# GpSimd issues the output stores of batches 1 to 7; the planner's SyncE lengths and its two strings are new

## The chip, the core and the metric

One core of one Trainium2 chip runs the whole program. The metric is device microseconds from start to end of one execution; smaller is better. The core has TensorE (matmul, "PE"), VectorE ("DVE"), ScalarE ("ACT"), GpSimd ("POOL") and SyncE ("SP"). SyncE, ScalarE and GpSimd issue the transfers, and sixteen DMA engines carry them. In the profile's rows, q1 is the ring of SyncE's transfers and q0 that of GpSimd's.

## The reference

Two layers follow each other on 8 batches of 3136 rows: a gated attention with squared ReLU in place of softmax, and a Hyena layer with an FFT convolution along the sequence.

```python
scores = (1.0 / S) * np.matmul(z, z.transpose(0, 2, 1))   # z: 8 x 3136 x 64
attn = np.maximum(scores, 0.0) ** 2
x = u * np.matmul(attn, v)                                # u, v: 8 x 3136 x 256
proj = x @ w_proj                                         # 256 -> 768
x1, x2, x3 = proj[..., :D], proj[..., D:2 * D], proj[..., 2 * D:]
x2_conv = np.fft.irfft(np.fft.rfft(x2, n=S, axis=1) * H, n=S, axis=1)
out = (x1 * x2_conv * x3) @ w_out                         # float32, 8 x 3136 x 256
```

H is the transform of `filter_fft`. S is 3136 = 64 x 49 and D is 256.

## The kernel before

All matmuls are in bfloat16 with float32 sums. The sequence is cut into seven chunks (`CHUNKS`: five of 512 rows, one of 256, one of 320), with rows laid out in the order that factors the Fourier transform into two small matrix products (64 x 49).

**Attention.** For each batch and chunk, TensorE makes scores between the chunk's rows and 128-row tiles of all rows (two tiles at a time, into a pair of PSUM banks; four such pairs exist). ScalarE or VectorE takes the ReLU into R_t (lines 1919 and 1921) and the square into A_t (1928 and 1930). TensorE weighs v with A_t and sums over the tiles. Since the scores are symmetric, a block made for one chunk is also needed, transposed, by a later one: `mirror` has SyncE transpose A_t into M_t, M2e_t or M2o_t by DMA (line 1848). At a chunk's end VectorE multiplies the sum with the transposed u (uT_t) into xT_t (line 1975).

**Loads.** GpSimd loads u, v and z and casts them to bfloat16 on the way (lines 621 to 656, into un_t, v_t, zn_t). It is paced: ahead of each load it copies one element of a finished tile (`tick`, lines 636 and 639), so that it waits until that tile is done. SyncE then transposes un_t into uT_t (line 1565) and the doubled z into zT_t (line 1620).

**Hyena.** From xT_t TensorE makes the three projections. The product of the first and third is the gate (gate_t, line 1256). The second goes through the first Fourier factor (`dft1`) and SyncE writes it to a DRAM scratch (`spec`, lines 1028 and 1031). When a batch's seven chunks are there, SyncE reads them back turned (spec_in_t, line 1062, three transfers per load), TensorE does the second factor, VectorE multiplies with H (xh, lines 1357 to 1362), TensorE transforms back (gs_t), and SyncE writes the result to the scratch (line 1406, three transfers each). `add_end` then handles one chunk at a time: SyncE loads conv_in_t (line 1091), TensorE finishes the inverse transform, VectorE applies the gate (yT_t, line 1462), TensorE multiplies with w_out, ScalarE or VectorE copies the float32 result into ost_t (lines 582 and 586), and a store goes to `out_dram` (line 1511). ost_t has two tiles. A store is two transfers, one for each half of the partitions.

**Order.** The program is one long straight list. While it is built, a planner (`Plan`) runs a clock: each piece of work is a `Task` with the engine, a planned length, what it depends on and which buffers it takes. A task with `moves` is a transfer: it lands later by its share of the DMA work, of which the planner keeps two heaps, SyncE's and GpSimd's; `late` is added to the landing. For SyncE, GpSimd, ScalarE and VectorE the planner picks the task that can start first on its clock (then the lower `prio`, then the older), and that fixes each engine's order of issue. For TensorE the order is written out in the string `ORDER`: one letter per piece (S scores, w and v the two halves of a weighing, A projections and first factor, Q spectrum, B the end of a batch, Z work kept for the last batch). The string `ENGINES` says for each piece that ScalarE (a) or VectorE (d) could do, which of them does it. All engines run in order, and each waits on semaphores for what it needs.

So the Hyena part of one batch is laid into the attention of the next. The stores of batches 0 to 5 are SyncE's; those of batch 6 are GpSimd's, four of them and three more inside the last batch; the last batch (7) divides its stores over GpSimd, SyncE and ScalarE. (The code counts batches from 0; batches 1 to 7 of the title are its 0 to 6.)

Of the kernel before, what the change touches and what calls it, by code (L numbers as in the profile page):

```python
# [27 lines left out]
LATE_U, LATE_ZT = 0.5, 2.0  # L28
# [28 lines left out]
    "vwSSwQwQAvAvSAvvwSAvwvSvwwwSvvQwwwSvSQvwAvQAvASvAQwwvSwvQwASAwvSwSwSvwASvSAwvAwSAvSwwwAvvASAvvAvvSSw"
    "wwSAvSAwvvSvASwAwwSBSBvwvSAvASwBvSBvAwAwABvBAwSvSwvAwAvSAvwSwwABSBwSvvAwAASAvwBvSBwAwABSwBvSvvSvvSwB"
    "ABvAwwSvwSwSAvBwABvvvSSwAwASvBvwBSwwAvSASwvwvBSBvwvASwAwwASAvQwvSQwvvSvQwwSQvwQvwQvSAvBABwAwBSAvBvvw"
    "SvSwwAASAwAvSvQwSwQwvSQvvvQwBwBwASvASwvwvSwwSvQvvwwvQSwwBvwSvBSvAvASAwASwvSSvvwQwQAvAwwvSASvSAwAQAwS"  # L60
    "wwQwSvASAvvwSwvvvSSvwvwvvwSAwSwASvwSvvAwBASBvwSwvSSwBvABvABvBwBwSBvSwvSAvwAwwSAvSAwvAwSAvBvBSvwSvAAA"
    "wABSwBwBAwwwBAAvAAvASvSvvvBABwASwwSwASAAvvSAvwvSBvSwwSwBSwSvwvSvSAvAvBQBwAvQwAvwQvwSvSQwAwwQAvvSvwQQ"
    "wwSvwAQvSAwvSwSvBwvSBvwvSAwAvvQSwBwBwQwBQvBQvvSvQwSSvwASwAvSvAwwAAwwvAvSvwwAvvwSvSAwSvwSwvBSwBAvSwAS"
    "vQSvwvvASwASwwwSQvvAwSSAwvSvwASvvSwwQwAvASAvwvvSvwwSAwASvvvwSSAvwAwAwSBABvvBwBSBwvSAvBAvSwAwASvvSBwS"
    "BvwwBwABvASvvSAwAwSSwBwBAvAASwAwBvBAAAvABSwvBSvwSvvSSvwBvBwwAwAvSSwwvvwAAAwSAvwSAvASSvwwvwSSQvvBwBQv"
    "vBSvBwwSvwAwAvwSSvAwAQvQvwSvQAwBABQwwvSvSQwBvwBAQAvSvvAQAwwAwQAvwSSvSwwvSSwAvvvSwQAvQwvSwQwwBSvQBvvS"
    "wvwwAvSvvwSvwwSAvQvwQvwSSvwSvAwSASvwAwSSAwwAwSASwvwvSSwvAwAvSAvASwwAvAvSvvSvwwvSwSvAvvAwBSBwvBwSBBBv"
    "wSvSAvAwwSSvvwSwSBvBwAvASvwwwSwBvBSAvAvvwwSwAAAAAvASwvSASwvBABSvvwSAvASwwwSwvwvvwSvSwvSSAwABvwvSwBSv"
    "wwSwSvwSBvBBvvBSvwvwASvAvwSwSAwASvAvAvSwASAwAvAQwvQwBvSwBQAwAwSvQAvwAwwQvvQvwSvQwABwBAQvwSvSQvvSwwQw"
    "BvSBvQvvSwSwwwvSvvvwwSAvSvAwwwSQvSvvSAwAvwSAvASASAQwSwwwQvSwQvASwASwvvwSwAvASvvwQSwwvAvAvSvvwSwwSABw"  # L70
    "BAvSvvSABABAwAwSSvvSvwASwASvwBSwBvwAwSAvSvAvAvSwBvwSBwAwAwAwSBABvvSAwAvSAwABSBwBvSvwBSvvvwSAvAAwABvB"
    "vwSwwSvSBwBvBvSwBvAwSAAvwSAwvSwBAwAwBAvASvvSwSAvASvAvAQwwSwQvwAQAvSwwwvSvASvwBASBvvwBQBvSwwQAwSAvSQv"
    "vvQwwSwSQwwwBvBQAvvASQvwSwwQvvwSQvvQwvSBwvSBvAvAAwAvwSSvwwwASAvvSwwwSQAwAvSQvvvSSvAwAwwSSwwwSASvAwSv"
    "wSvvQwSvvwASvwvAAwSvvAvvwSwwSAwSAvvBwSBBwBSvAwAvSSvwSwABvSABvwSBwSvBvwvSSBvBAvAwwwSABwABvvSvSBvBSwwA"
    "AAASvAwASAvAwSAwAwBSvBBvBwSvwSvwwSwSvvSvwvASwAwSwwBSvSBwwQQvSvvwQSvAvwQAvBvQBvwwvQAwAwwQwQSvwvSSvvvB"
    "BvBBvwSwASwwSAvSvwSvvSwvvAwASwSvwvBSvwwBQwQAvSAwvQwSvwQQvwSvwAQvSAvwvwBvSvwBwwASAwvvSSwvAQvwAvSwQvvS"
    "wwwSSvAwASvwwZvSZAwAvSvvwwwZwwZvvvvvvZZABABZZAABBBBZZZZBZBZBZZZZBQQQQBQQQBQQQQQZZQQZQZQZZZZZBZBZZZBZ"
    "BBZBBZBZBBBBBZBBBBBZZZZBBBBBBBBBBBBBB"
# [3 lines left out]
    "aadddddddaaddaaaaaaddaaaddaadaadaadadadadaaaadadaddadddaaaadaadaaddaadaadaaddaddaaaaaaaaadadaddaddad"  # L82
    "aaaadadaaadaddadadaaaadddaaadaaaaddaddaaaaddaaadadddaaaaaaadadaaaaaadddaaadadaaaaaaaaadaaaaaddaadadd"
    "aaddaadadaaaadadadaddaaadaaadaaddaddadadaaddadadaadaaaddaadaaaadaddaaaaaddddadaaadaaaaaddaadaaaaaada"
    "addadaadaddaaadadaaaadaaaadaadaaaaddddaadadaaaaaaadaaaaddaaadaaadddaadaadaaadadadaaadddaaadaaaadddad"
    "adaaaaadddadadadaaaadaaaadddaaaaaaddaadaddaadaaadaaaaaadadaaddaaaaaadaaadaaadaadaaaaaaaadaaddaaaaaaa"
    "aaaaaaaadddadadadaaadadaadaaaaaadaaaaaaaaaaaaadddaaddaaaadadaddadaaaaadddaaaadddaaaddaaaddaaaaaaaaaa"
    "dadaaaadaddaaadaadddaaaaadaaadaddadadaaaaaaadadaadaaaaadaaadadadaaadaadaadddaddaadaaddaadadaddadadaa"
    "adadaaaaadaaaaaddadadaddaadaaaadaadaaadaaadadadaaadadaaaaadddaadaaaadaaaaaaddadddaaaadaadaaaddaaaaad"
    "aaaaaadaaaaaaaaaadaddadaddaaaadaaaaadaadadddaaaddaaddaaaaddadaadaaddaaaadaaaaddaaaadaaaaaadadaddaada"  # L90
    "aaaaaddadaadadadadaaaaddaaadadaaddadadaaaadadaaddadadaaaaaaaddadadaaaddaaddaaaaaadaaaadaaaaaaadadaad"
    "adaaaaadadadaddadadaaaddaaadaaaaadaaaaaaaaaaadaaaaaaaaadaaaadddaaddadaadaadaaaadadaddddadaaaaadaddda"
    "adaaaadddaaddaaaaaaaaaaddaaaddaadaadaaadaadaadaaaadadaadaddaaaadaddadaaaaadaaadadaaaaadaddadaaaadaaa"
    "addddaddadaaaadaadaadaaaadaaadaaaadaddadaaddaaadddaaaaaaaaddaadadadadddadaaaaaaaadaaadadadaaaaddaada"
    "dddaaadaaadaaaadaaaaaddaadaddaaaddaaadaadaadaddaaaaaadddaaadaadaadddaaddaaaadadaaddaaaaaaadaaaaaaaaa"
    "aaaaaaaadaaaaaaaaaaadadaad"
# [3 lines left out]
ISSUED = "issued"  # L100
# [286 lines left out]
def kernel(  # L387
# [188 lines left out]
    def on(engine, emit, cost, deps=(), takes=(), **kw):  # L576
        return job(None, lambda e: emit(), {engine: cost}, deps, takes, **kw)
# [420 lines left out]
    def dft1(kind, get, t0, nt, dst, deps, free=None, late=0.0, split=False):  # L998
# [40 lines left out]
        c = on("SP", put, 0.5 * (1 + (nt == 3)), [b_], moves=0.254 * nt, late=late)  # L1039
# [5 lines left out]
    def in_order(task):  # L1045
        loads.append(task)
        return task
# [8 lines left out]
    def load_spec(src, j0, nj, deps, late=0.4, home=l_p):  # L1056
        box = {}

        def go():
            box["t"] = home.tile([P, 8, D], BF16)  # L1060
            for rows, part in by_row(src, box["t"], 2 * j0, 2 * nj):
                nc.sync.dma_start(out=part, in_=rows)
# [21 lines left out]
    def load_c(src, c, deps, home):  # L1084
# [8 lines left out]
        if home is c_p:  # L1093
            return in_order(on("SP", go, 0.55, [*deps, *((d, ISSUED) for d in loads[-1:])], [home.slots], moves=0.254 * nt, late=LATE_C)), box
# [224 lines left out]
    def add_spectrum(b, puts, early=0):  # L1319
# [10 lines left out]
        for g in range(NJ // 2):  # L1330
# [41 lines left out]
            def inv(g=g, xb=xb, z_=z_, a0=a0, gh=gh, mine=mine, per=per):  # L1372
# [41 lines left out]
                else:  # L1414
                    p_ = on("SP", put, 1.5, gx["es"], moves=0.389 * per, late=LATE_D2)
# [10 lines left out]
    def add_end(b, lasts, gtasks, cs, kind="FB", src=c_p, dsts=(o_p,), late=0, behind=(), then=(), split=False, mids=(y_p,)):  # L1426
        for at, c in enumerate(cs):
# [92 lines left out]
            elif b == B - 2:  # L1520
# [40 lines left out]
    def load_uT(b, c, deps):  # L1561
# [9 lines left out]
        if not isinstance(made[0], Task):  # L1571
            t = after(on("SP", go, 1.3, deps, [uT_p.slots], moves=0.2 * u_tiles(c), late=LATE_U), made[1])
# [497 lines left out]
```

## Time and profile before

| | |
|---|---|
| three runs | 950.38, 957.36 and 955.5 us; median 955.5 |
| profiled execution | span 944.1 us from the first to the last instruction; its own time with what lies around the span is not listed |
| granted TensorE clock | 0.997 of full speed |
| HBM | read 90.26 MB, written 53.05 MB |
| chain that ended last | TensorE 77%, DMA 10%, VectorE 6%, ScalarE 3% |

The page gives busy time per engine, a chain of waits followed back from the last instruction, and groups of instructions. A matmul's end is modelled, so short waits can be hidden in TensorE's busy time. SyncE's issues are not counted as busy; their lengths stand in the timeline and in the rows of a line or tile. "DMA share" is the sum of the packets' times over sixteen engines, and can pass 1. The page's TensorE row of the 40 slices reads 9 nearly throughout:

```profile
PE   8999999999999999999999999999999999999986
```

### The profile page before, as it was taken

What the parts mean: (1) busy time and instruction counts of PE and PEld (TensorE: products, weight loads), DVE (VectorE), ACT (ScalarE), POOL (GpSimd) and SP (SyncE); (2) the same over time, 40 slices, a digit from 0 to 9 for tenths busy, and PEclk for the clock granted to TensorE, in tenths of its full rate; (3) what the DMA queues carried; (4) which work ended last, traced back from release to release, by engine and by line L of the source; (5) the groups of instructions that cost most, each with busy time, mean ns of one, the idle gap of its engine ahead of it and who ended that gap; (6) DMA issues with size and microseconds to landing.
All of it is one profiled execution on the core that took longest, in us unless ns stands there. A gap on an engine that the chain in (4) does not pass through costs nothing.

```text
span 944.1 us, 30298 instructions
## 1 busy us (share of the span) xinstructions
PE 914.1 (97%) x12423; PEld 557.1 (59%) x12423; DVE 838.5 (89%) x1116; ACT 819.7 (87%) x953; POOL 248.8 (26%) x585
## 2 busy tenths in 40 slices
PE   8999999999999999999999999999999999999986
PEld 3446565566555666556665665666665666666654
DVE  8987899998888998999888988989988999899785
ACT  7968988999889988888989998889988999899573
POOL 5244223231322322223121321333123140101030
PEclk9999999999999999999999999999999999999999
DMA  9999799978999889998899989999889989897867
GB/s 155 162 181 181 117 179 184 181 150 182 170 217 201 146 181 192 209 156 159 190 183 215 176 155 200 173 184 174 183 172 207 221 138 196 193 216 132 193 189 241
DMA packets 331643, 170.70 MB, mean 181 GB/s; under 512 B 242886, under 2 KB 307142, under 8 KB 331504
## 3 DMA queue, kind: packets, MB, share of 16 engines
q1 hardware_dynamic: 301624, 131.98, 70.1%
q0 software_dynamic: 29168, 35.13, 26.4%
q8 instruction: 97, 1.59, 0.7%
q10 hardware_dynamic: 712, 1.66, 0.6%
q14 instruction: 42, 0.34, 0.1%
HBM read 90.26 MB, written 53.05 MB: 152 GB/s over the span
## 4 chain that ended last, share of the span: by engine, by line
PE 77%; DMA 10%; DVE 6%; ACT 3%; issue 2%; SPq 1%; POOL 0%; ACTq 0%; DVEq 0%; POOLq 0%
PE ps_s L516 77%; DMA M_t<-A_t 4%; DMA out_dram<-ost_t 1%; ACT R_t L1919 1%; DMA M_t<-spec_in_t 1%; DVE xh L1357 1%; ACT A_t L1928 1%; DVE yT_t L1462 1%; DVE A_t L1930 1%; DMA v_t<-spec 1%; DMA spec<-gs_t 1%; DMA M2e_t<-A_t 1%; ACT gs_t L582 1%; DVE R_t L1357 1%; DMA spec_in_t<-spec 0%
## 5 line engine op out<-in xcount | busy, mean ns | idle before, releaser
L516 PE MATMUL ps_s<-A_t,v_t 64*128 64x512 bf16 (+5 forms) x4766 | 516.1, 352 | 0.9 <-DVE A_t L1930 0.7
L516 PEld LDWEIGHTS <-v_t 64*128 64x128 bf16 (+1 forms) x6528 | 306.4, 98 | 187.7 <-PE ps_s L516 19.3
L1919 ACT ACTIVATE R_t<-ps_s 128x1024 f32<-128x1024 f32 (+3 forms) x359 | 336.9, 962 | 47.4 <-PE ps_s L516 43.8
L1928 ACT ACTIVATE A_t<-R_t 128x1024 bf16<-128x1024 f32 (+2 forms) x281 | 271.8, 993 | 15.3 <-DMA M_t<-A_t 6.3
L1930 DVE SCALAR_TENSOR_TENSOR A_t<-R_t 128x1024 bf16<-128x1024 f32 (+3 forms) x211 | 233.6, 1123 | 21.6 <-ACT R_t L1919 12.1
L516 PE MATMUL ps_s<-zT_t 64*128 64x512 bf16 (+5 forms) x1186 | 192.2, 351 | 3.6 <-DVE gate_t L1256 2.1
L1921 DVE TENSOR_SCALAR R_t<-ps_s 128x1024 f32<-128x1024 f32 (+4 forms) x153 | 170.2, 1123 | 20.9 <-PE ps_s L516 10.4
L639 POOL COPY tick<-A_t 1x1 bf16<-1x1 bf16 x159 | 56.2, 354 | 428.0 <-ACT A_t L1928 264.2
L516 PE MATMUL ps_s<-xT_t,wp 64*128 64x512 bf16 (+3 forms) x976 | 124.7, 352 | 0.1
L516 PE MATMUL ps_s<-M_t,v_t 64*128 64x512 bf16 (+4 forms) x860 | 97.2, 353 | 3.2 <-DMA M_t<-A_t 2.4
L516 PEld LDWEIGHTS <-zT_t 64*128 64x128 bf16 (+1 forms) x1219 | 69.1, 97 | 51.7 <-issue 8.2
L582 ACT ACTIVATE x_t<-ps_s 128x1024 bf16<-128x1024 f32 (+3 forms) x75 | 69.5, 928 | 22.8 <-PE ps_s L516 22.5
L1357 DVE TENSOR_TENSOR xh<-xh,H 128x1024 bf16<-128x1024 bf16 x120 | 81.7, 685 | 2.3 <-ACT xh L582 1.4
L1256 DVE TENSOR_TENSOR gate_t<-ps_s,x_t 128x512 bf16<-128x512 f32 (+2 forms) x112 | 64.4, 617 | 12.4 <-PE ps_s L516 9.0
L1462 DVE TENSOR_TENSOR yT_t<-ps_s,gate_t 128x1024 bf16<-128x1024 f32 (+2 forms) x53 | 56.9, 1078 | 14.3 <-PE ps_s L516 14.1
L1975 DVE TENSOR_TENSOR xT_t<-ps_s,uT_t 128x512 bf16<-128x512 f32 (+2 forms) x112 | 64.0, 613 | 6.3 <-PE ps_s L516 5.8
L516 PEld LDWEIGHTS <-wp 64*128 64x128 bf16 (+1 forms) x976 | 48.0, 96 | 29.7 <-PE ps_s L516 2.0
L516 PE MATMUL ps_s<-wp,xT_t 64*128 64x256 bf16 (+2 forms) x944 | 64.2, 266 | 0.8 <-ACT R_t L1919 0.7
L516 PE MATMUL ps_s<-wo,yT_t 64*128 64x256 bf16 (+2 forms) x904 | 62.1, 266 | 2.2 <-DVE yT_t L1462 1.0
L625 POOL DMA_DIRECT2D un_t<-in_u_dram x112 | 57.9, 518 | 17.4 <-issue 15.6
L651 POOL DMA_DIRECT2D v_t<-in_v_dram x112 | 58.2, 524 | 14.1 <-issue 10.4
L516 PEld LDWEIGHTS <-xT_t 64*128 64x128 bf16 (+1 forms) x944 | 44.1, 97 | 19.3 <-issue 1.5
(156 smaller groups left out, 905.7 us busy)
## 6 DMA issues: line engine op xcount, KB each, us to landing
out_dram<-ost_t SPq DMA_DIRECT2D x60, 256.0 KB
spec_in_t<-spec SPq DMA_DIRECT2D x56, 192.0 KB
spec<-gs_t SPq DMA_DIRECT2D x56, 192.0 KB
v_t<-in_v_dram POOLq DMA_DIRECT2D x80, 128.0 KB, 4.8
un_t<-in_u_dram POOLq DMA_DIRECT2D x80, 128.0 KB, 4.4
spec<-s_t SPq DMA_DIRECT2D x40, 256.0 KB
conv_in_t<-spec SPq DMA_DIRECT2D x34, 256.0 KB
out_dram<-ost_t SPq DMA_DIRECT2D x18, 128.0 KB
```

Source lines behind the costliest of these rows:

```text
L516: got = nc.tensor.matmul(o, *args, **kw)
L582: got = nc.scalar.activation(out_, in_, AF.Copy)
L625: nc.gpsimd.dma_start(out=t[ds(j * N1, N1), lo - t0 : hi - t0, :], in_=x[:, n2 : n2 + hi - lo, :])
L651: nc.gpsimd.dma_start(out=t[ds(j * N1, N1), ds(v_at(a), (b - a) * D)], in_=r[:, n2 + a - lo : n2 + b - lo, :].rearrange("p t d -> p (t d)"),)
L1256: has_read(nc.vector.tensor_tensor(o[:, :, ::-1] if h == 0 else o, p, x, ALU.mult), p)
L1357: nc.vector.tensor_tensor(x[:, 1 - i], x[:, 0], h, ALU.mult)
L1462: has_read(nc.vector.tensor_tensor(yb["y"][:, :, 0:w], p, gates[b, c][:, :, 0:w], ALU.mult), p)
L1919: has_read(nc.scalar.activation(r, p, AF.Relu), p)
L1921: has_read(nc.vector.tensor_single_scalar(r, p, 0.0, ALU.max), p)
L1928: nc.scalar.activation(a, r, AF.Square, scale=1.0 / float(S))
L1930: nc.vector.scalar_tensor_tensor(a, r, inv_s2, r, ALU.mult, ALU.mult)
L1975: has_read(nc.vector.tensor_tensor(x[:, :, ::-1] if h == 0 else x, f, ut, ALU.mult), f)
```

## The change

It has three parts. In `add_end`, the branch that hands a store to GpSimd takes all batches but the last, where it took batch 6 alone. The GpSimd task has a planned length of 1.2 us, priority 0 and no added lateness; the SyncE task that it replaces had 1.1 us, priority 1 and 0.5 us of lateness. The planned lengths of five kinds of SyncE tasks are raised, in six places; no instruction comes from that. And both strings are replaced. `ORDER` has 2637 letters before and after, each letter as often; `ENGINES` has 1426, of which 939 were ScalarE's before and 935 are after. The first 16 letters of `ORDER` agree; after that the two orders differ all along.

```diff
 ORDER = (
-    "ASSAwSSvAwSSAwwSSvvwSBvwSvSwvSvwSwSvvSwSSvwwSvvwwSvwAvSwAwwSvSvSAvvwwSwwSvvvSABwvBwwSvvAwAvSSwwvSSwA"
...
+    "ASSAwSSvAwSSAwwSvSvvSwBSvwwSvSwvSvSwwSvSvSwwSvvwwwwSAvAwSvwSvwSvSvAwvSwvSvASwvvwBSBvAvAwwSvSwwwvwSw"
...
 ENGINES = (
-    "aadddddddaaddaaaaaaddaaaddaadaadaadadadadaaaadadaddadddaaaadaadaaddaadaadaaddaddaaaaaaaadadaddaddad"
...
+    "aadddddddaadaaddaaadadaaadaaadaadaadadadadaaaadaddadadadaadaaddaaaaadaaddddaaaaaaaaddaadaddaaaaddada"
...
@@ dft1: the first factor's result to the scratch
-        c = on("SP", put, 0.5 * (1 + (nt == 3)), [b_], moves=0.254 * nt, late=late)
+        c = on("SP", put, 0.7 * (1 + (nt == 3)), [b_], moves=0.254 * nt, late=late)
@@ load_spec: the scratch read back
-        t = on("SP", go, 1.5, [*deps, *((d, ISSUED) for d in loads[-1:])], [home.slots], moves=0.389 * nj, late=late)
+        t = on("SP", go, 1.95, [*deps, *((d, ISSUED) for d in loads[-1:])], [home.slots], moves=0.389 * nj, late=late)
@@ load_c: one chunk for the end of a batch
-            return in_order(on("SP", go, 0.55, [*deps, *((d, ISSUED) for d in loads[-1:])], [home.slots], moves=0.254 * nt, late=LATE_C)), box
+            return in_order(on("SP", go, 0.7, [*deps, *((d, ISSUED) for d in loads[-1:])], [home.slots], moves=0.254 * nt, late=LATE_C)), box
@@ add_spectrum: the back transform's result to the scratch
-                    p_ = on("SP", put, 1.5, gx["es"], moves=0.389 * per, late=LATE_D2)
+                    p_ = on("SP", put, 2.1, gx["es"], moves=0.389 * per, late=LATE_D2)
@@ add_end: the output stores
-            elif b == B - 2:
+            elif b < B - 1:
                 s_ = on(
                     "POOL", lambda nt=nt, store=store: store(0, nt, by=nc.gpsimd), 1.2, [*oe, *behind],
                     moves=0.508 * nt, late=LATE_POOL,
                 )
@@ load_uT: the transposes of u (two places)
-            t = on("SP", go, 1.3, [*deps, *made], [uT_p.slots], moves=0.2 * u_tiles(c), late=LATE_U)
+            t = on("SP", go, 1.4, [*deps, *made], [uT_p.slots], moves=0.2 * u_tiles(c), late=LATE_U)
```

The branch that the stores of batches 0 to 5 took before is

```python
            else:
                s_ = on("SP", lambda nt=nt, store=store: store(0, nt), 1.1, [*oe, *behind], prio=1, moves=0.508 * nt, late=LATE_OUT * (dst is o_p))
```

More of the change, by code (lines that the diff above doesn't have):

```diff
@@ L57 @@
[L57 to L66, printed above, removed]
@@ new lines @@
+    "wASwvAvQQAwwSvwQvSQvAvASAvwAwwSwvvASAwAwSAQvwASwQAvwSvQvQvvSwvAQAAwASvQwwwvSvQvwSvwQwSwSvAQvAwSwvQvQ"
+    "SvwwvSAvwSvwASAwAvvwvSvwSwwSvvvQwwSSvvQAwwSAQvAwSAwQvwwvSvQwSAvAvSwSvwwSASvAvvASwASvwwwwASAAvAvSvvSw"
+    "wSvAwASAwAvwBSSvvBSwvSvwwBSSvvBwAAwAwASvBvBASAvwSvwAvASAwAvSwSvAwSAwBvSABwwAwBAvBwSAwBSBvSwSvvSSvvwB"
+    "vBwSvwwwSAvwAAvAwvSvSvBSwBBwwBSwvAvSvSAwvBSvAwAvvwBwSvAAAwAwQSwSvwQBwwAQABvvvSQwvQAvSAvQvSwBwwSBvSvv"
+    "wSwAvSvAAwASwvQwSQvwvSQvwwSQvvwSBAvwBwSwAvSvvBwwwBQvvwQvwSSvwSvSAvAwwASwASvvSvQQwwAvASAvAwwSvvwSQvQw"
@@ L97 @@
+    "aaaaaaaaaaaaaaaadaaaddaaaa"
 )
@@ L1571, in load_uT @@
         if not isinstance(made[0], Task):
-            t = after(on("SP", go, 1.3, deps, [uT_p.slots], moves=0.2 * u_tiles(c), late=LATE_U), made[1])
+            t = after(on("SP", go, 1.4, deps, [uT_p.slots], moves=0.2 * u_tiles(c), late=LATE_U), made[1])
             t.frees.append((Held(un_p.slots, made[0]), 0))
         else:
-            t = on("SP", go, 1.3, [*deps, *made], [uT_p.slots], moves=0.2 * u_tiles(c), late=LATE_U)
+            t = on("SP", go, 1.4, [*deps, *made], [uT_p.slots], moves=0.2 * u_tiles(c), late=LATE_U)
             t.frees.append((made[0], 0))
```

67 lines of the change are left out of this document (36 added, 31 removed).

## The prediction

> **What bounds the kernel now.** I read the page's busy shares first, then the table of windows, then the chain of waits, and last the SyncE queue's own timeline.
>
> ```profile
> span 944.1 us, 30298 instructions
> ...
> PE 914.1 (97%) x12423; PEld 557.1 (59%) x12423; DVE 838.5 (89%) x1116; ACT 819.7 (87%) x953; POOL 248.8 (26%) x585
> ...
> q1 hardware_dynamic: 301624, 131.98, 70.1%
> q0 software_dynamic: 29168, 35.13, 26.4%
> ```
>
> TensorE is busy for 914.1 of 944.1 us, so an edit that leaves its work alone can win at most the 30 us in which it stands still, plus short waits that its modelled ends cover. The two DMA rows add to 96.5% of the sixteen engines' span: DMA has almost nothing spare either. The next rows say where the 30 us lie. Columns: length of the stretch, busy time (instructions) of each engine, granted clock, DMA share, GB/s.
>
> ```profile
> 50.00:850.00 800.00, 789.59 (x10719) 485.57 (x10716) 720.67 (x928) 716.74 (x813) 212.98 (x504) 1.00 1.00 181
> 850.00:944.00 94.00, 79.94 (x1333) 51.99 (x1329) 72.37 (x103) 61.04 (x92) 15.60 (x32) 0.99 0.77 190
> ```
>
> In 800 us of steady running TensorE loses 10.4 us; the tail from 850 us loses 14.1 us; the remaining 5.4 us are the start. The steady loss is not spread out. Four stretches, each where one batch's spectrum work meets the next batch's attention, hold nearly all of it:
>
> ```profile
> 286.00:296.00 10.00, 7.93 (x87) 4.34 (x83) 7.34 (x12) 8.09 (x11) 3.65 (x8) 1.00 1.13 197
> 384.00:412.00 28.00, 25.38 (x403) 13.86 (x401) 24.52 (x38) 24.44 (x28) 7.69 (x18) 1.00 1.25 209
> 500.00:508.00 8.00, 6.37 (x72) 3.58 (x70) 6.48 (x12) 6.08 (x7) 3.03 (x8) 1.00 1.17 196
> 616.00:664.00 48.00, 45.13 (x769) 31.36 (x765) 42.92 (x67) 42.75 (x52) 14.20 (x35) 1.00 1.09 183
> ```
>
> They lose 2.07, 2.62, 1.63 and 2.87 us, 9.2 us together, at a DMA share of 1.09 to 1.25. The timeline of the SyncE queue (start, length, what is issued) ahead of the first of them:
>
> ```profile
> 275.94 1.40 SPq L1565 DMA_TRANSPOSE uT_t<-un_t  x1
> 277.44 4.15 SPq L1511 DMA_DIRECT2D out_dram<-ost_t  x4
> 281.68 2.30 SPq L1062 DMA_DIRECT2D spec_in_t<-spec  x3
> 284.09 1.26 SPq L1848 DMA_TRANSPOSE M2o_t<-A_t  x1
> 285.46 2.68 SPq L1848 DMA_TRANSPOSE M_t<-A_t  x2
> 288.25 2.46 SPq L1406 DMA_DIRECT2D spec<-gs_t  x3
> ```
>
> SyncE issues without a pause, and four output stores hold it for 4.15 us while the spectrum loads, the transposes of mirrored blocks and the spectrum stores stand behind them. So TensorE is the bound, and what stops it at the batch borders is late data from a full SyncE queue and full DMA engines.
>
> **The change part by part.** First, the stores of the first six batches leave SyncE: seven chunks of two transfers, 84 issues (the seventh batch's stores are on GpSimd already).
>
> ```profile
> L1511 SPq DMA_DIRECT2D out_dram<-ost_t x84: 466/586/1927, 232.0 to 872.3; - x84
> L1511 POOL DMA_DIRECT2D out_dram<-ost_t x8: 518/526/547, 894.1 to 924.5; - x8
> ```
>
> At the median (middle of the three ns figures) that is 84 x 0.586 = 49 us of SyncE's time, more where it is crowded. Most of it is worth nothing, because TensorE did not wait there. It counts in the four stretches. Ahead of the first it is the 4.15 us above. The others, as that line's rows in the windows 370 to 400 and 600 to 664 us and one row of the timeline:
>
> ```profile
> L1511 SPq DMA_DIRECT2D out_dram<-ost_t x4: 588/750/1462, 386.8 to 393.8; - x4
> ```
>
> ```profile
> L1511 SPq DMA_DIRECT2D out_dram<-ost_t x6: 527/938/1477, 617.2 to 648.9; - x6
> ```
>
> ```profile
> 493.79 0.50 SPq L1511 DMA_DIRECT2D out_dram<-ost_t  x1
> ```
>
> That frees about 4 x 0.75 = 3.0 us in the second, 0.5 in the third and 6 x 0.94 = 5.6 in the fourth. A stall cannot give more than it is, nor more than SyncE is freed by: the upper bound is 2.07 + 2.62 + 0.50 + 2.87 = 8.1 us. The lower bound is nothing, if the data are late for the DMA engines' sake. The chain of waits chooses between these (two answers: from 277 us, and from 370 us):
>
> ```profile
> 278.99 0.62 SPq L1511
> 279.61 0.05 issue
> 279.66 5.55 DMA out_dram<-ost_t
> ```
>
> ```profile
> 399.80 7.75 DMA M_t<-A_t
> ...
> 497.44 7.33 DMA M_t<-A_t
> ...
> 636.50 0.79 SPq L1062
> 638.34 5.61 DMA spec<-gs_t
> ```
>
> In the first stretch the chain runs through the store's own issue and landing, in the fourth through SyncE's issue of a spectrum load right behind a pair of stores. In the second and third it runs through transposes that take 7.75 and 7.33 us from the start of their issue until they land, which no shorter queue mends. I count the first and fourth in full and the others at nothing: 2.07 + 2.87 = 4.9 us. What is late next in these stretches is the transposes' landing.
>
> The Trainium skill speaks against a larger gain: its page "DMA: Bandwidth & Descriptors", section "Issuing engines are not separate DMA queues", says that transfers from SyncE, ScalarE and GpSimd run on the same sixteen engines and interleave, so that spreading the issues saves only the sequencer's time. By that rule alone the DMA share of 1.09 to 1.25 stays, and the sum would lie between the 4.9 us and nothing.
>
> Second, GpSimd takes the 84 issues: 84 x 0.526 = 44 us on top of 248.8, some 31% of the span. It also takes the wait for each eviction, and it is in order: behind a waiting store stand the small copies (tick) that pace the casting loads of u, v and z, and these loads; for u SyncE's transpose uT waits, and for uT the VectorE product at a chunk's end. What covers it:
>
> ```profile
> L639 POOL COPY tick<-A_t 1x1 bf16<-1x1 bf16 x159 | 56.2, 354 | 428.0 <-ACT A_t L1928 264.2 <-DVE A_t L1930 163.2
> ...
> L636 POOL COPY tick<-xT_t 1x1 bf16<-1x1 bf16 x54 | 10.0, 184 | 158.5 <-DVE xT_t L1975 158.2
> ```
>
> ```profile
> L1565 SPq EVENT_SEMAPHORE  x66: 17/28/7176, 7.1 to 880.0; - x66
> ```
>
> GpSimd stands 428.0 + 158.5 us waiting for its own pace marks, and SyncE's wait ahead of a uT transpose is 28 ns in the median: u is mostly there long before. I take 0; the bounds are 0 and the third rival's price. The store itself lands no sooner: in the tail GpSimd's stores take this from issue to landing (min/median/max us),
>
> ```profile
> DMA to landing us min/median/max: 3.2/3.7/6.3
> ```
>
> against 5.55 us for SyncE's store above in a crowded stretch. The output buffer has two tiles, so the second covers it; if that cover goes, an output eviction waits 1 to 3 us. Transfers of 256 KB, 60 of the 84, leave ring q1 for q0:
>
> ```profile
> out_dram<-ost_t SPq DMA_DIRECT2D x60, 256.0 KB
> ```
>
> That is over 15 MB of q1's 132; the bytes and the engines stay the same, so I count 0 for bandwidth.
>
> Third, the planner's costs of SyncE's tasks rise. They add no instruction; they tell the planner, which lays out the order of issue on all engines but TensorE and the choice of evicting engine, that SyncE is fuller. Fourth, the two strings. TensorE's has the same letters as often as before (512 S, 648 w, 648 v, 424 A, 229 B, 136 Q, 40 Z), so its work is the same; the other moves four of 1426 pieces from ScalarE to VectorE, about 4 x 838.5/1116 = 3 us of an engine that has 105 us idle. The new order has no price in this trace. Outside the four stretches only 10.4 - 9.2 = 1.2 us is left to win before 850 us, and in the tail I bound the gain by a fifth of 14.1 us, 2.8. On the other side, an order may leave new stalls; the nearest row is what the present one leaves, 9.2 us. Between +9.2 and -4 I take 0, because the pieces and the tail's form are the same.
>
> **Sum.** 4.9 us off a span of 944.1 gives 939.2 us. That execution's own time is not listed; its span lies 6.3 to 13.3 us below the three runs (950.38 to 957.36), 11.4 below their median of 955.5. Against that median the forecast is 955.5 - 4.9 = 950.6 us, 0.5% less. A measurement of this kernel can tell about 1%, 9.6 us, from no change.
>
> **The rivals.**
> (a) *Nothing measurable comes back*: the data are late because the DMA engines are full. For it speak the share of 1.09 to 1.25 in all four stretches and transposes of over 7 us; against it the unbroken SyncE queue. Time: 955.5 us. The Trainium skill's rule above gives the same where the issue time was not what counted.
> (b) *More than forecast*: with SyncE's real lengths in the plan all four stretches close, and the new order wins its 2.8 us in the tail: 955.5 - 8.1 - 2.8 = 944.6 us, or less where short waits under TensorE's modelled ends go too. Against it: the chain's landings in two stretches.
> (c) *Late loads, slower*: a store that waits on GpSimd for its eviction holds the next u load, uT is late, and TensorE stops at a chunk's end. The nearest row is what SyncE waited for u already:
>
> ```profile
> SPq L1565 <- DMA un_t<-in_u_dram: 13.8, 5, 7.2
> ```
>
> Five waits, 2.8 us each. One such wait per batch that reaches TensorE in full costs 6 x 2.8 = 16.6 us; less the 4.9, the time is 955.5 + 11.7 = 967.2 us. It eats the gain from 0.8 us per batch and makes the kernel slower by over 1% from (4.9 + 9.6)/6 = 2.4 us per batch. Against it: the 28 ns median.
> (d) *VectorE holds GpSimd's descriptors*, slower: an issue may have to wait out a VectorE operation.
>
> ```profile
> L1357 DVE TENSOR_TENSOR xh<-xh,H 128x1024 bf16<-128x1024 bf16 x120 | 81.7, 685 | 2.3 <-ACT xh L582 1.4
> ```
>
> Were each of the 15 stores in and ahead of the four stretches held for one such operation, and TensorE with it, that is 15 x 0.685 = 10.3 us: 965.8 us. Against it: the GpSimd stores above take 518 to 547 ns, a spread of 29 ns, though the tick copies differ (354 against 184 ns in the mean). The Trainium skill's page "SBUF — State Buffer", section "Who interferes with whom", has the rule: GpSimd and certain VectorE operations share one pair of ports, and the second to come is blocked for the whole instruction. The 29 ns do not show it on these issues.
>
> **How the numbers follow.** Forecast 0.46, (a) 0.21, (b) 0.20, (c) 0.10, (d) 0.03. The predicted time is the forecast's 950.6 us; its own range is 947.4 (all 8.1 us) to 955.5 (none). The range 942 to 961 us takes in the forecast and (a), about half of (b), down past 944.6, and the mild part of (c) and the order's loss of 9.2 - 4.9 = 4.3 us, up to 959.8: about 0.8. Faster by over 1% (below 946) is (b) and a tenth of the forecast, where the order adds to it: 0.25. Slower by over 1% (above 965) is nearly all of (c) and (d): 0.12. The rest, 0.63, is within 1%.
>
> **What would show it.** Right: no out_dram row for SyncE before the last batch, 92 ost_t stores on GpSimd, TensorE's loss from 50 to 850 us down from 10.4 to 5 or 6 us, the stretches that remain ending in transposes' landings, SyncE's wait for u not above 13.8 us, a DMA share as before. Wrong: TensorE's loss unchanged with SyncE idle (a), SyncE's wait for u doubled (c), GpSimd's store issues well above 0.55 us (d), or new stalls where no store ever stood, which would be the new order's.

## The result and the profile after

The changed kernel takes 963.72 us (median of 7 runs, 959.6 to 966.62) beside 952.48 us before (7 runs, 949.46 to 957.36). The ratio is 1.0118, with a 95% interval of 1.0086 to 1.0149: it became slower, where the prediction had 0.5% less, and the time lies above the range. The ratios here and below leave out runs that lie over 1.5% above the fastest of their kernel, so they can differ a little from the quotient of the medians. The profiled execution of after took 966.62 us, with a span of 964.8 us, 20.7 more than the profiled span of before; its granted clock is 0.981, against 0.997. These two profiles overstate the loss: a run's time is some 1.8 us longer than its span, so the profiled execution of before took some 945.9 us, less than each of the seven, and that of after is the longest of its seven. They differ by 20.7 us where the medians differ by 11.2.

From the page of after: span, busy time, the two DMA rings, and two of its groups of instructions: ScalarE's squares and GpSimd's stores.

```profile
span 964.8 us, 30279 instructions
...
PE 923.4 (96%) x12425; PEld 563.0 (58%) x12425; DVE 835.3 (87%) x1121; ACT 823.4 (85%) x948; POOL 290.2 (30%) x669
...
q1 hardware_dynamic: 294904, 112.71, 64.8%
q0 software_dynamic: 35120, 54.41, 33.7%
...
L1928 ACT ACTIVATE A_t<-R_t 128x1024 bf16<-128x1024 f32 (+4 forms) x276 | 269.6, 996 | 26.8 <-DMA M_t<-A_t 12.0
...
L1511 POOL DMA_DIRECT2D out_dram<-ost_t x92 | 48.9, 537 | 122.2 <-ACT ost_t L582 87.5
```

The stores moved as the change says: 92 on GpSimd at 537 ns, 19 MB from ring q1 to q0, the sum of the two rings' shares 98.5% where it was 96.5%. GpSimd is busy for 30%. ScalarE's squares (L1928) stood 12.0 us for DMA transposes of M_t, where it had been 6.3. The windows of after (length, busy us and instructions of PE, PEld, DVE, ACT and POOL, granted clock, DMA share, GB/s):

```profile
50.00:850.00 800.00, 779.20 (x10505) 477.20 (x10505) 703.14 (x909) 706.70 (x795) 251.54 (x581) 0.99 1.03 176
850.00:964.80 114.80, 100.03 (x1561) 66.68 (x1552) 88.53 (x130) 78.08 (x108) 18.86 (x40) 0.93 0.79 189
```

TensorE's loss in the steady 800 us doubled, from 10.4 to 20.8 us. It also has another shape. Before, TensorE's longest single wait in this stretch was 2.07 us; after, four long ones hold 18.3 of the 20.8. The timeline of TensorE, the first matmul after each (idle time before it, and what ended it, in brackets):

```profile
84.08 1.03 PE L516 MATMUL ps_s<-M_t,v_t 64*128 64x512 bf16 x4 [6.55 <-DMA M_t<-A_t]
```

```profile
398.24 1.06 PE L516 MATMUL ps_s<-M2o_t,v_t 64*64 64x512 bf16 x16 [2.97 <-ACT ost_t L582]
```

```profile
510.77 0.39 PE L516 MATMUL ps_s<-zT_t 64*128 64x512 bf16 x2 [3.75 <-DVE xh L586]
```

```profile
740.78 1.04 PE L516 MATMUL ps_s<-wp,xT_t 64*128 64x256 bf16 x8 [5.07 <-ACT R_t L1919]
```

The engines named in three of them are not the cause, only the last link. The chain of waits of after has a transpose ahead of all four: of M_t at the first, second and fourth, of M2o_t at the third:

```profile
69.99 14.04 DMA M_t<-A_t
84.03 0.05 issue
84.08 36.03 PE ps_s L516 x414
```

```profile
387.16 8.98 DMA M_t<-A_t
```

```profile
499.34 8.32 DMA M2o_t<-A_t
```

```profile
729.67 8.99 DMA M_t<-A_t
...
738.76 0.06 ACT A_t L1928
...
739.72 1.01 ACT R_t L1919
740.74 0.04 issue
740.78 29.67 PE ps_s L516 x446
```

Read the last one downwards. A transpose of A_t into M_t is issued at 729.67 and lands 8.99 us later. Only then is its source tile A_t free, so ScalarE's next square can write there (738.76); ScalarE is in order, so the ReLU behind it (739.72) runs only then and empties a PSUM pair; then TensorE goes on (740.78).

**The stalls cost twice.** After each, the granted clock is 0.50 for some microseconds. The windows of after over these stretches; the fifth is in the tail; the same rows' sum follows:

```profile
82.00:88.60 6.60, 4.52 (x22) 1.63 (x24) 1.38 (x2) 0.88 (x1) 0.28 (x2) 0.50 0.87 131
399.20:402.60 3.40, 3.40 (x40) 1.99 (x36) 2.08 (x4) 2.76 (x3) 2.89 (x6) 0.50 1.07 285
512.00:515.30 3.30, 3.27 (x22) 1.53 (x19) 3.26 (x7) 2.30 (x3) 0.00 (x0) 0.50 1.03 310
740.60:744.00 3.40, 3.22 (x24) 2.00 (x25) 0.00 (x0) 1.63 (x3) 2.06 (x4) 0.50 1.10 235
921.50:935.10 13.60, 12.44 (x192) 9.08 (x193) 11.79 (x21) 12.01 (x23) 3.75 (x7) 0.50 0.58 156
sum 30.30, PE 26.85 PEld 16.23 DVE 18.52 ACT 19.58 POOL 8.99; mean PE 5.37 PEld 3.25 DVE 3.70 ACT 3.92 POOL 1.80
```

Between start and end, the trace of before has no such stretch. The two pages split the 20.7 us: TensorE stands still for 41.4 us where it stood for 30.0, and is busy for 923.4 us where it was 914.1, with the same work. So 11.4 us are added waits and 9.3 us are slower matmuls. An estimate from the windows comes out higher: at half the clock, 26.85 us of matmuls hold work for half of that, 13.4 us.

The Trainium skill's page "TensorE: Matmul & The Clock Gate", section "🎯 Why this matters for your kernels", asks for no idle gap of TensorE above some 3 us between bursts, since one idle window brings the half clock back. This trace agrees: the four waits are of 2.97 us and more, the half clock follows each in stretches of 3.4 or 6.8 us, and before, with 2.07 us as the longest, has none. The other runs show no sharp bound: half clock followed every wait of 3.50 us or more in mid-run, also one of 2.06 us in e2 (at 415 us) and one of 2.23 us in e8 (at 399 us), but not one of 3.26 us in e9 (at 76 us).

### The profile page after: what moved, and what is told of

Its sections match the earlier page's. It is cut to its first block, busy times and chain, and to the rows that moved or that the text cites. A ratio compares the mean times of both kernels' runs of the same rounds, so it can differ in the third digit from the quotient of the medians.

```text
span 964.8 us, 30279 instructions
## 1 busy us (share of the span) xinstructions
PE 923.4 (96%) x12425; PEld 563.0 (58%) x12425; DVE 835.3 (87%) x1121; ACT 823.4 (85%) x948; POOL 290.2 (30%) x669
## 3 DMA queue, kind: packets, MB, share of 16 engines
q0 software_dynamic: 35120, 54.41, 33.7%
## 4 chain that ended last, share of the span: by engine, by line
PE 82%; DMA 10%; DVE 3%; ACT 3%; issue 1%; SPq 0%; POOL 0%; DVEq 0%; ACTq 0%; POOLq 0%
PE ps_s L516 82%; DMA M_t<-A_t 5%; DMA M2o_t<-A_t 2%; DMA M_t<-spec_in_t 1%; ACT R_t L1919 1%; DVE A_t L1930 1%; DMA spec<-s_t 1%; DMA spec_in_t<-spec 1%; ACT ost_t L582 0%; DMA A_t<-spec 0%; DVE xh L1357 0%; DMA out_dram<-R_t 0%; ACT A_t L1928 0%; DMA out_dram<-v_t 0%; DVE gate_t L1256 0%
## 5 line engine op out<-in xcount | busy, mean ns | idle before, releaser
L516 PEld LDWEIGHTS <-v_t 64*128 64x128 bf16 (+1 forms) x6498 | 304.9, 98 | 201.7 <-PE ps_s L516 23.2
L1919 ACT ACTIVATE R_t<-ps_s 128x1024 f32<-128x1024 f32 (+2 forms) x361 | 336.7, 960 | 50.5 <-PE ps_s L516 45.8
L1928 ACT ACTIVATE A_t<-R_t 128x1024 bf16<-128x1024 f32 (+4 forms) x276 | 269.6, 996 | 26.8 <-DMA M_t<-A_t 12.0
L1930 DVE SCALAR_TENSOR_TENSOR A_t<-R_t 128x1024 bf16<-128x1024 f32 (+1 forms) x216 | 236.5, 1115 | 17.0 <-ACT R_t L1919 7.6
L516 PE MATMUL ps_s<-zT_t 64*128 64x512 bf16 (+5 forms) x1191 | 194.9, 355 | 5.3 <-DVE xh L586 3.7
L1921 DVE TENSOR_SCALAR R_t<-ps_s 128x1024 f32<-128x1024 f32 (+3 forms) x151 | 167.4, 1120 | 35.9 <-PE ps_s L516 31.8
L639 POOL COPY tick<-A_t 1x1 bf16<-1x1 bf16 x159 | 49.4, 311 | 333.9 <-ACT A_t L1928 217.4
L516 PEld LDWEIGHTS <-zT_t 64*128 64x128 bf16 (+1 forms) x1224 | 71.9, 98 | 55.0 <-issue 12.2
L1511 POOL DMA_DIRECT2D out_dram<-ost_t x92 | 48.9, 537 | 122.2 <-ACT ost_t L582 87.5
L1462 DVE TENSOR_TENSOR yT_t<-ps_s,gate_t 128x1024 bf16<-128x1024 f32 (+2 forms) x53 | 57.0, 1079 | 11.6 <-PE ps_s L516 10.4
```

Source lines behind the costliest of these rows:

```text
L516: got = nc.tensor.matmul(o, *args, **kw)
L1462: has_read(nc.vector.tensor_tensor(yb["y"][:, :, 0:w], p, gates[b, c][:, :, 0:w], ALU.mult), p)
L1919: has_read(nc.scalar.activation(r, p, AF.Relu), p)
L1921: has_read(nc.vector.tensor_single_scalar(r, p, 0.0, ALU.max), p)
L1928: nc.scalar.activation(a, r, AF.Square, scale=1.0 / float(S))
L1930: nc.vector.scalar_tensor_tensor(a, r, inv_s2, r, ALU.mult, ALU.mult)
```

## The experiments

All ratios are to runs of the kernel before on the same chip, with 95% intervals. Its median was 950.47 us for e1 to e4 (29 runs), 949.95 for e5 to e8 (16), 948.32 for e9 to e12 (17) and 949.67 for e13 to e16 (29). Each run has one profiled execution, and a step in it need not be there in the others of that kernel.

**One part at a time.** The first run leaves the order of before as it is, to the letter, on every other engine, and only names GpSimd as the issuer:

```diff
-                s_ = on("SP", lambda nt=nt, store=store: store(0, nt), 1.1, ...
+                s_ = on("SP", lambda nt=nt, store=store: store(0, nt, by=nc.gpsimd), 1.1, ...
```

> The order of before, kept to the letter on TensorE, VectorE, ScalarE and SyncE; only the engine that issues the 84 stores of the first six batches is GpSimd. Theory R (ring): the stores' bytes on GpSimd's ring compete with SyncE's transposes, which land later, so this part alone costs time: ratio to before 1.006 to 1.015, and stretches at half clock that before does not have. Theory O (order): the two strings and not the stores make the loss; the freed SyncE gives the forecast's 2 to 5 us: ratio 0.995 to 0.999, no new half-clock stretches.

The second is the changed kernel, its order as planned, with SyncE as the issuer at the same places:

```diff
-                    "POOL", lambda nt=nt, store=store: store(0, nt, by=nc.gpsimd), 1.2, ...
+                    "POOL", lambda nt=nt, store=store, by=nc.gpsimd if b == B - 2 else nc.sync: store(0, nt, by=by), 1.2, ...
```

> The order of the changed kernel on all engines, but SyncE issues the stores of the first six batches, at the places where the new plan has GpSimd issue them. Theory R: the loss goes, ratio to before 0.99 to 1.002. Theory O: the loss stays or grows, since the new order counts on a SyncE without stores: ratio 1.010 to 1.025, with the half-clock stretches near 82, 400, 512 and 740 us still there.

The third and fourth keep the stores on SyncE, in the plan too. One takes the new lengths of SyncE's tasks with the old strings, the other the new lengths and both new strings.

> Both strings and the stores as before; only the planned lengths of SyncE's tasks are the new ones, which moves the order of the other engines a little. Theory O, that an order chosen for other lengths does not fit: ratio 1.003 to 1.02. Theory R: 0.997 to 1.003.

> New lengths and new strings, the stores planned and issued on SyncE. Theory R: ratio 0.99 to 1.002. Theory O: 1.005 to 1.03.

> The changed kernel once more, so that it stands beside the next three. Every theory: ratio to before 1.008 to 1.015. Theory G (steps): set against the plan's own clock, its vector products at the chunks' ends fall back in a few steps of 5 us or more at the places of the first profile (batch 0 chunk 4, batches 3, 4 and 6 at chunks 2 to 4), since the order is fixed and the late transposes are always the same ones. A rival, chance: the steps stand elsewhere each time.

| kernel | median us | ratio | interval |
|---|---|---|---|
| e1, stores alone | 947.11 | 0.9982 | 0.9946 to 1.0018 |
| e2, order alone | 953.8 | 1.0033 | 0.9998 to 1.0068 |
| e3, lengths alone | 966.83 | 1.0152 | 1.0082 to 1.0222 |
| e4, lengths and strings | 955.78 | 1.0058 | 1.0027 to 1.009 |
| e5, the change again | 963.45 | 1.0115 | 1.0058 to 1.0172 |

So the two parts do not add. Moving the issue costs nothing in the old order (e1); the new order with SyncE's issue costs a third of a per cent (e2), with an interval that just takes in no change; together they cost 1.1%. Of the two theories neither is enough: e1 falls in theory O's range, e2 in neither's. The new lengths without new strings (e3) are the worst of all: the strings were written for lengths, and a plan made of the one with the other is no measure of the lengths in a plan of their own. The old lengths with the new strings were not run.

The first run also answers the prediction's sum. The windows of that run at the prediction's four stretches:

```profile
286.00:296.00 10.00, 8.22 (x90) 4.58 (x88) 8.30 (x14) 8.36 (x11) 2.85 (x7) 1.00 1.14 198
384.00:412.00 28.00, 27.60 (x473) 16.29 (x472) 27.12 (x43) 26.13 (x29) 11.04 (x26) 1.00 1.18 223
500.00:508.00 8.00, 8.00 (x111) 4.70 (x111) 7.61 (x12) 7.97 (x9) 4.64 (x9) 1.00 1.28 185
616.00:664.00 48.00, 45.16 (x778) 30.63 (x775) 43.73 (x69) 43.31 (x53) 15.83 (x36) 1.00 0.99 179
```

The second and third stretch, where the chain ran through transposes' landings, closed (loss 2.62 to 0.40, 1.63 to 0). The first and fourth, which had SyncE's issues in the chain, kept theirs (2.07 to 1.78, 2.87 to 2.84). SyncE's rows ahead of the third and of the fourth say why; first before, then e1:

```profile
490.28 4.00 SPq L1511 DMA_DIRECT2D out_dram<-ost_t  x2
495.41 5.09 SPq L1848 DMA_TRANSPOSE M_t<-A_t  x2
619.18 5.71 SPq L1848 DMA_TRANSPOSE M_t<-A_t  x2
```

```profile
490.69 5.44 SPq L1848 DMA_TRANSPOSE M_t<-A_t  x2
616.33 8.07 SPq L1848 DMA_TRANSPOSE M_t<-A_t  x2
```

At the third stretch the pair of transposes is issued no faster without the stores, but 4.7 us sooner, and the stall is gone. At the fourth the pair starts 2.9 us sooner and takes 2.4 us longer, so it ends where it did. The first is like the fourth: its pair starts at 284.58 instead of 285.46 and takes 4.42 us instead of 2.68. Added up over the whole execution, the stores had held SyncE for 56.9 us, and in e1 its 260 transposes take 23.2 us longer to issue (447.5 us, before 424.3). The new order shows the same: 433.5 and 430.2 us with SyncE's stores (e2, e15), 450.4 to 464.3 with GpSimd's (after, e5, e16). So some of what SyncE gains it pays back, because the stores then run beside its transposes.

**Is it the traffic or the issue?** Two runs do not write the results of the first six batches, two write the first half of the rows of each of these stores, with as many issues as before. The edits, for the changed kernel and for before alike:

```diff
-                    if j in only:
+                    if j in only and b >= B - 2:
```

```diff
+                        m_ = (hi - lo + 1) // 2 if b < B - 2 else hi - lo
-                        by.dma_start(out=r[:, n2 : n2 + hi - lo, :], in_=ob["o"][ds(j * N1, N1), i0 : i0 + hi - lo, :])
+                        by.dma_start(out=r[:, n2 : n2 + m_, :], in_=ob["o"][ds(j * N1, N1), i0 : i0 + m_, :])
```

> The changed kernel without the output stores of the first six batches (their results are not written); all else in the same order. Theory S: in the new order the stores on GpSimd's ring delay SyncE's transposes at the batch borders, so the steps of batches 3, 4 and 6 go and the step of batch 0, ahead of any store, stays: ratio to before 0.995 to 1.004. Theory O (order): the transposes are late without the stores too: ratio 1.006 to 1.012.

> The kernel before without the output stores of the first six batches (not written). It bounds what any other way of storing can give in this order. My forecast priced it at 4.9 to 8.1 us: ratio 0.991 to 0.995. A rival: nothing, 0.997 to 1.001, if the transposes' landing and not SyncE's issue time holds TensorE.

> The changed kernel, where each store of the first six batches writes only the first half of its rows (rounded up; the other half is not written): as many issues, waits and pieces as before, half the bytes. Theory T (traffic): the price of a store is its bytes beside the transposes, so the ratio to before lies midway between 1.0115 (full) and 0.9888 (none), 0.997 to 1.004, and the steps of batches 3, 4 and 6 are half as high or gone. Rival I (issues): what counts is each store's issue and wait on GpSimd: 1.008 to 1.013.

> The same halving in the kernel before, whose stores SyncE issues. Theory T: midway between 1 and 0.984, 0.990 to 0.994. Rival I (SyncE's issue time, as my forecast priced it): 0.997 to 1.001, since SyncE issues as many transfers for as long.

| kernel | median us | ratio | interval |
|---|---|---|---|
| e6, changed, without these stores | 941.26 | 0.9888 | 0.9855 to 0.9921 |
| e7, before, without them | 934.57 | 0.984 | 0.9795 to 0.9885 |
| e9, changed, half the rows | 939.01 | 0.9902 | 0.9864 to 0.9939 |
| e10, before, half the rows | 936.89 | 0.9891 | 0.9851 to 0.993 |

It is the traffic and not the issues. In the old order half the bytes bring back 1.1 of the 1.6% that the stores cost, though SyncE issues as many transfers for as long (584 ns in the median, 586 in before) and ring q1 carries as many packets (301624); midway between 1 and 0.984 lies inside the interval. In the new order nearly all comes back: 0.9902 against 0.9888, more than theory T expected. Why half is so much more than half the gain there was not settled; the packets on GpSimd's ring fall with the bytes, from 35120 to 32912.

So the stores cost 1.6% of the time in the old order, whichever engine issues them (e1), and about 2.3% in the new one (1.0115 - 0.9888). Without any of them, e6 and e7 lie below what was expected of them, and the new order is still about half a per cent slower than the old (0.9888 against 0.984), though these intervals overlap.

**Where the new order breaks first.** At 77 us, in the first batch, no output store has run yet, and TensorE stands for 6.55 us. The queues of after around it, SyncE and GpSimd:

```profile
67.20 8.21 SPq L1848 DMA_TRANSPOSE M_t<-A_t  x2
```

```profile
63.25 1.23 POOL L725 DMA_DIRECT2D xh<-in_moe_filter_fft_dram  x2 [0.66 <-issue]
64.52 0.31 POOL L729 MEMSET gate_t<- 64x256 bf16 x1
64.78 0.52 POOL L730 DMA_DIRECT2D gate_t<-in_moe_filter_fft_dram  x1
65.28 0.74 POOL L731 DMA_DIRECT2D wo<-in_moe_w_out_dram  x1
66.00 1.57 POOL L625 DMA_DIRECT2D zn_t<-in_z_dram  x3
67.53 0.57 POOL L651 DMA_DIRECT2D v_t<-in_v_dram  x1
```

Before has the same loads within half a microsecond of the same places, and its pair of transposes took 4.03 us:

```profile
67.17 4.03 SPq L1848 DMA_TRANSPOSE M_t<-A_t  x2
```

So the loads' burst is not enough by itself; in the new order the pair takes 8.21 us, and TensorE waits for it. Every kernel with this order has the wait: 3.50 us in e6, 3.26 in e9, 4.07 in e15, 5.32 in e2. What in the order makes the pair so slow was not found. e8 issues the last part of the filter and w_out together with the part before, some 16 us earlier.

```diff
-    filt_ld = [Task(lambda e, x=x: load_filter(*x), {"POOL": 1.6}, moves=4.2, late=2.0) for x in filt_cuts]
+    filt_now = ((filt_cuts[0],), filt_cuts[1:], ())
+    filt_ld = [Task(lambda e, xs=xs: [load_filter(*x) for x in xs], {"POOL": 1.6}, moves=4.2, late=2.0) for xs in filt_now]
```

> The changed kernel, where GpSimd issues the third part of the filter (with w_out) right behind the second, one chunk earlier, so that it is not beside the transposes of batch 0 chunk 3. Theory F: the burst of GpSimd loads at 63 to 68 us makes these transposes late, and the step of 9 us at batch 0 chunk 4 goes: ratio to the changed kernel 0.990 to 0.994. Rival: the transposes are late by themselves, the step stays or moves one chunk ahead: 0.998 to 1.002.

The time stayed (963.32 us, 1.0128, 1.0082 to 1.0175), as the rival expected. The stall moved with the burst, one chunk earlier, which the rival allows too: the run shows the stall beside the burst at both places, and not that the burst alone makes it. SyncE and TensorE of that run:

```profile
53.96 6.29 SPq L1849 DMA_TRANSPOSE M_t<-A_t  x2
60.34 5.80 SPq L1849 DMA_TRANSPOSE M2e_t<-A_t  x1
```

```profile
70.02 1.89 PE L516 MATMUL ps_s<-M_t,v_t 64*128 64x512 bf16 x8 [7.29 <-DMA M_t<-A_t]
```

**Are the stores' long packets the cause?** If rings take turns packet by packet, longer runs in GpSimd's stores would crowd out the transposes, and short ones would not. e11 and e12 name the rows of a store in reverse on both sides, so that the rows no longer follow each other in one run and each run is one row (1 KB).

```diff
+                        if b < B - 2:
+                            o_, x_ = o_[:, ::-1], x_[:, ::-1]
```

> The changed kernel, where the stores of the first six batches name their rows in reverse order on both sides, so that a partition's 4 KB go as four runs of 1 KB; issues, bytes and all orders as in the changed kernel. Theory P (packets): the DMA engines alternate between the two rings packet by packet, and the transposes' packets of some 0.3 KB lose to stores of several KB; with short runs the transposes land sooner and the ratio to before falls from 1.0115 to 1.000 to 1.008. Rival: bytes count and not runs: 1.009 to 1.014; or shorter runs take the engines longer, 1.014 and more.

> The same short runs where only the store's issuing engine is changed (order of before, stores on GpSimd). Theory P: faster than with whole rows, ratio to before 0.990 to 0.997. Rival: 0.997 to 1.002, or slower than 1.002 if short runs cost the engines time.

The changed kernel took 961.4 us (1.0145, 1.01 to 1.019), the stores alone 949.45 (1.0019, 0.9989 to 1.0049). Nothing came back. But this does not decide the theory, because the packets stayed as they were. The GpSimd ring on the page of e11:

```profile
q0 software_dynamic: 35216, 54.41, 34.4%
```

After has 35120 packets for the same bytes, and in both traces nearly all of the stores' packets are of 4 KB. Stores in shorter packets were not tried.

**Where GpSimd's issue is paid.** The last four kernels ran side by side on one chip. A store of batch b runs two batches later, so the five stores below, of batches 1 and 4, run in batches 3 and 6. e13 takes five of the 42 stores back to SyncE, those right beside two of the long stalls; e14 leaves only these five on GpSimd; e15 and e16 are e2 and the changed kernel again.

```diff
-                    "POOL", lambda nt=nt, store=store: store(0, nt, by=nc.gpsimd), 1.2, ...
+                    "POOL", lambda nt=nt, store=store, by=nc.sync if ((b == 1 and c in cs[2:5]) or (b == 4 and c in cs[2:4])) else nc.gpsimd: store(0, nt, by=by), 1.2, ...
```

> The changed kernel, but five of its 42 stores are issued by SyncE at the same place of the plan: those that run right beside the steps at some 390 us (batch 1, chunks 2 to 4) and at some 730 us (batch 4, chunks 2 and 3). Theory L (the price of GpSimd's issue is paid at those two steps, because the stores' traffic then runs beside SyncE's transposes instead of standing behind them): of the 7.8 us between the changed kernel (1.0115) and the new order with SyncE's issue (1.0033), at least 5 come back, 1.003 to 1.006, and the steps at 390 and 735 us shrink below 3 us each. Theory S (each store on GpSimd costs a little wherever it stands): 5/42 of 7.8 us, 0.9 us, come back, 1.0106, and the steps stay.

> The complement: the changed kernel with all stores of the first six batches issued by SyncE, but for the same five, which stay on GpSimd. Theory L: most of the 7.8 us is lost, 1.0085 to 1.0115, with steps of over 4 us at 390 and 735 us. Theory S: 0.9 us over the order alone, 1.0043, and no step at 735 us.

> The changed kernel with SyncE issuing all stores of the first six batches, once more, beside the two runs above on one chip. Both theories: 1.0033 as before; it is the lower mark for the two runs above.

> The changed kernel once more, beside the runs above on one chip. Both theories: 1.0115 as before; it is the upper mark for the two runs above.

| kernel | median us | ratio | interval |
|---|---|---|---|
| e13, all but five on GpSimd | 955.15 | 1.0037 | 1.0004 to 1.007 |
| e14, only five on GpSimd | 956.16 | 1.0073 | 1.0035 to 1.0111 |
| e15, order alone again | 955.06 | 1.0058 | 1.0021 to 1.0095 |
| e16, the change, third time | 960.27 | 1.0106 | 1.0056 to 1.0155 |

e13 is as fast as the order alone (e15), so 37 of 42 stores cost nothing measurable on GpSimd once those five are back on SyncE, and theory S's 1.0106 lies outside its interval. The intervals of e15 and e16 overlap, but all six times of e16 (958.35 us and more) lie above e15's median. e14 lies between the two theories, and its interval holds values of both. The places tell more than the times. The start of the product at a chunk's end (line 1975), later than in e6, which has the same order and not the stores, in us:

```
batch, chunk             0,4    3,2    3,3    4,1    4,2    6,2    6,3    7,6
after                    4.8    6.8   11.6   11.3   16.7   15.3   22.0   24.5
the change, second       6.3   11.2   17.7   17.4   23.3   22.1   26.9   28.9
the change, third        2.3    6.1   12.3   12.0   17.7   16.5   16.5   20.4
e14, only five on GpSimd 3.7    6.4    8.0    8.2   16.9   18.9   24.6   24.7
e13, five on SyncE       1.0    6.9    8.9   10.3   16.8   15.6   15.9   16.1
e15, order alone         5.6    7.8    8.1    8.6   15.5   14.1   14.1   14.1
e2, order alone          2.5    5.5    7.0   10.6   18.2   17.3   18.0   18.5
e9, half the rows       -2.2   -1.0   -1.0   -1.3   -1.3   -1.8   -1.8   -1.2
```

A step is where a row jumps between neighbours. At (4,2) all kernels with whole stores lose 5 to 9 us, whoever issues them: that step is the new order's, and with half the bytes it is gone. At (6,3), some 735 us, e14 loses 5.7 us and two of the three executions of the change 6.7 and 4.8; e13, e15 and e2 lose under 1, and so does the third execution of the change, so that the step is likely there and not certain. The profiled execution of e14 took 963.57 us, 7.4 more than the median of its kernel. At (3,3) the change loses 4.8 to 6.5, e14 only 1.6, e13 2.0: neither the five stores alone nor the other 37 alone bring this one about.

What differs at (6,3) stands in the queues. In e14, as in after, SyncE issues a pair of transposes at once while GpSimd's store runs (SyncE, then GpSimd):

```profile
732.90 5.55 SPq L1848 DMA_TRANSPOSE M_t<-A_t  x2
```

```profile
731.06 1.05 POOL L1511 DMA_DIRECT2D out_dram<-ost_t  x2 [0.90 <-ACT ost_t L582]
732.10 0.53 POOL L625 DMA_DIRECT2D un_t<-in_u_dram  x1
```

In e13 the same store is in SyncE's queue, and so between the two transposes:

```profile
727.81 1.29 SPq L1848 DMA_TRANSPOSE M_t<-A_t  x1
729.20 1.18 SPq L1511 DMA_DIRECT2D out_dram<-ost_t  x2
730.70 2.07 SPq L1848 DMA_TRANSPOSE M_t<-A_t  x1
```

One queue puts the first transpose ahead of the store; two queues let the store and the load run beside both, and the pair took 5.55 us to issue where 1.29 and 2.07 had done. This holds in every profiled execution of these kernels: the two issues add up to 4.92 to 6.52 us with GpSimd's store (after, e5, e16, e14) and to 2.64 to 3.55 with SyncE's (e15, e13, e2). The third execution of the change (e16) has 5.10 us and no step here, so the long issue comes each time, and TensorE need not come to wait for it. TensorE's busy time in the window 732 to 746 us, e14 and then e13:

```profile
732.00:746.00 14.00, 9.77 (x93) 4.96 (x91) 7.07 (x9) 7.37 (x8) 3.75 (x10) 0.89 1.19 204
```

```profile
732.00:746.00 14.00, 13.74 (x200) 9.53 (x200) 12.41 (x16) 11.78 (x14) 3.86 (x10) 1.00 1.18 232
```

None of the kernels that compute the whole result beats the one before beyond its interval; e1 is nearest (0.9982).

## Why the prediction was wrong

- *TensorE is the bound, late data stop it*: right, before and after.
- *First, SyncE freed, 4.9 us*: too large, and for the wrong stretches. Alone in the old order it gave 0.18% (0.54% less to 0.18% more, 5.1 us less to 1.7 more at 950 us), 1.7 us in the middle; the 4.9 us lie at the edge of that. The two stretches that the prediction counted in full kept their loss; the two that it counted at nothing, because a landing of over 7 us is one "which no shorter queue mends", closed. This reading of the chain is a step that failed: the shorter queue did not make the transposes faster, but let the pair of the third stretch start 4.7 us sooner. The 0.50 us freed there was one row of two; the two stores had held SyncE for 4.00 us. And in the two stretches counted in full, the time freed went into transposes that took 1.7 and 2.4 us longer to issue.
- *Second, "the bytes and the engines stay the same, so I count 0 for bandwidth"*: this is the step that turned the sign, together with the fourth. The bytes stay; their order against the transposes does not. In the new order GpSimd's issue cost 0.48% more than SyncE's in runs side by side (1.0106 against 1.0058, 4.6 us) and 0.82% between e5 and e2, though in the old order nothing (e1). The upper bound "nor more than SyncE is freed by" was drawn for a gain; no bound was drawn for a loss here. The rule that the prediction cites there, from the Trainium skill's page "DMA: Bandwidth & Descriptors", section "Issuing engines are not separate DMA queues", is that issues from several engines save only the sequencer's time. The old order agrees with it (0.9982, no measurable gain). In the new order leaving the queue also gave up the order within it.
- *Second, GpSimd's 84 issues at 0*: right. The issues took 536 ns in the median, 680 at most, so rival (d) is out. Rival (c), late loads, had a time near the measured one (967.2) by luck, by a mechanism that did not decide: SyncE waited 17.0 us ahead of uT in 7 waits, where it had been 13.8 in 5, and none of the four long stalls ends in uT. Rival (a) would have left the time alone, and (b) had the wrong sign.
- *Third and fourth, the new lengths and strings at 0, between +9.2 and -4*: mis-sized, within these bounds. Together they measured +0.33% and +0.58% (3.1 and 5.5 us, e2 and e15). The bounds were drawn in idle time alone. That stalls bring half the clock behind them, 9.3 us of slower matmuls in the profiled execution, stood in no row of before.
- *What stays open*: which transposes the new order makes late, and why, beyond the places shown; and why the five stores alone on GpSimd (e14) cause only a part of the loss that taking them away from it (e13) saves.
- *What would show it wrong*: the prediction named "new stalls where no store ever stood", and the stall at 77 us is one. It gave the kernel a chance of 0.12 to be slower by over 1%.

## What to carry to other kernels

A transfer that is taken out of a full queue is not only issued elsewhere, it also stops standing in line: look at what stood behind it in that queue, and price the case that both run at once, above all where a buffer's release hangs on the other transfer. Where a kernel is within 1 or 2% of its bound, one stall of TensorE of some 3 us or more can cost more than several short ones of the same sum, because half clock can follow (in the middle of these runs it did after every wait of 3.50 us or more). Try the move in the old order and the new order with the old issuer, before judging either: here the one was free and the other cost 0.3 to 0.6%, and both together 1.1%.

## What the runs showed of the hardware

- The issue of one M_t transpose by SyncE took 1.3 us in the median, before and after, and 5.4 us in after behind GpSimd's burst of loads (at 70 us); pairs beside GpSimd's transfers took 4.0 to 8.2 us. A transpose landed 8.3 to 14.0 us after the start of its issue at the four long stalls, and 7.3 to 7.8 us after it at two stalls of before. In the new order half the rows in the stores took nearly all of the stores' price away, in the old one two thirds.
- The half clock came in steps of 3.4 us: 3.4 to 10.2 us after a stall in the middle (10.2 in e5, after a wait of 8.42 us), and 13.6 us in the tail of the profiled execution, although TensorE was busy there for all but 1.2 us. What holds it there was not tried, nor was the clock's share of the loss measured by a run of its own.
